# Building the routing tables on GpSimd, reading them in three operations, and splitting the first expert's weights earlier

## The chip, the cores and the metric

The kernel runs on one core of a Trainium2 chip. A core has a matrix engine (TensorE, PE in the profile), a vector engine (VectorE, DVE), a scalar engine (ScalarE, ACT), a general engine (GpSimd, POOL) and SyncE (SP), which here only issues transfers. The engines run side by side, each through its own list of instructions in order, and wait for one another by semaphores. Data lies in HBM, in the on-chip memory SBUF (128 partitions) and in PSUM, where TensorE writes its results. The metric is the device time of one execution in microseconds; lower is better.

## The reference, cut to what matters

```python
B, H, S, D = 8, 8, 576, 64        # attention, window of 64
scores = 0.125 * q @ k.T          # kept where 0 <= row - column < 64
attn = exp(scores - max) / (sum + 1e-9)
x = (attn @ v) as [4608, 512]     # one row per token
logits = x @ w_gate               # 8 experts
e = argmax(logits); gate = softmax(logits)[e]
out[token] = gate * (relu(x @ w1[e]) @ w2[e])   # w1[e]: 512x1024, w2[e]: 1024x512
```

All of it is float32. Each token goes through the one expert that its logits choose, so the kernel must sort tokens by expert.

## The kernel before, in words

**The attention loop.** 4,608 rows are 36 tiles of 128. The main loop runs 43 steps; step i works on several tiles at once, as a pipeline written out by hand: TensorE makes the scores of tile i; VectorE folds them into one window and finds the maximum (`folded`, `largest`); ScalarE takes the exponentials of tile i-1 (`exps`), TensorE transposes them (`transp`), ScalarE copies them out of PSUM (`evac`, tile `tsb`) and GpSimd splits them by two masks (`apart`: two operations `pm` of 128x512, for tile i-2); TensorE multiplies by v (`values`, tile i-3), VectorE divides (`shares`, tile `xrow`, sent to HBM as `xs`), TensorE transposes the rows (`rows_t`, tile i-4), ScalarE copies them (`xT`), and TensorE computes logits. There is one PSUM buffer for most of these, so each engine's list, which is in the order of the code, sets what waits for what. SyncE loads the 72 chunks of q, k and v four steps ahead of their use.

**The routing.** It runs in three rounds, over 14, 12 and 10 tiles. A round (`route`) is a chain of small operations s1 to s8, at most three in a step. s8 ends with each token's place in its expert's list, split into a block number `mid` and a row in the block `lo`, and with the gate `g` split into three bfloat16 parts in `val`. Then `put` makes one-hot rows: `hot_row[:, t]` is 128x128, with a one where the column number equals `lo`. `parts` multiplies, for each wanted block, a mask `here` with five numbers of each token (its partition, its tile, three parts of the gate), giving `said`; TensorE multiplies `said` by `hot_row` (`gathered`, L608), which gives for each place in a block the token and its gate; `read` turns that into an index and a gate. With the index GpSimd gathers rows of `xs` (`fetch`, L172). After round 1 two blocks each of experts 0 and 1 are gathered ahead, after round 2 those of experts 2 and 3; after round 3 a plan is made for all other blocks, with one big table of 32 columns, and passes over them follow until the end.

For round 1, s1 to s3 stand at the end of step 18, s5 to s7 in step 20, s8 and the first two `put`s in step 21, two more `put`s in step 22, `parts` in steps 23 and 24, the table and `read` at the beginning of step 25, the gathers in steps 26 and 27.

**The experts.** From step 29 on TensorE also works on the first expert. Products are made in three passes of single-pass format: a weight tile `raw` is rounded by ScalarE (`whi`, L231) and the remainder taken by VectorE (`wlo`, L228). The first two of these splits for expert 0 are made ahead, each in four pieces of 128x256, one piece in each of steps 20 to 27 (`SPLIT`, `prepare`, `pieces`). Their 8 quarter loads of 256 KB each stand in SyncE's list in steps 18 to 25 (`LOADW`, `quarters`, L850).

## Time and profile before

| what | value |
|---|---|
| median of 3 runs (lowest, highest) | 669.79 us (667.69, 670.86) |
| time of the profiled execution | 670.64 us |
| its span, first to last instruction | 668.8 us |
| PE busy | 618.6 us, 93% |
| DVE busy | 414.2 us, 62% |
| ACT busy | 359.8 us, 54% |
| POOL busy | 193.0 us, 29% |
| DMA | 138.14 MB, mean 207 GB/s |

The attention loop fills the first 205 us or so, mixed with expert work from about 130 us on; from 260 us to the end TensorE works through the experts. A line of the timeline gives start, duration, engine, line of the kernel, operation, what it writes and reads, shapes, and in brackets how long the engine sat idle before it and who ended that. Busy shares are means over stages that have different limits, so a stage is read by itself.

### The profile page before, as it was taken

The numbers are of one execution on the slowest core, as the hardware profiler recorded it, in microseconds if no ns is written. First come the engines' busy times: TensorE is split into PE (matmuls) and PEld (weight loads), VectorE is DVE, ScalarE is ACT, GpSimd is POOL, SyncE is SP. The second block draws the span as 40 slices with busy tenths as digits, with TensorE's granted clock in tenths as the row PEclk, the third lists the DMA queues.
The fourth block names the chain that finished last, engine by engine and source line by source line (L and its number), as shares of the span: only waits on it lengthen the run. The fifth ranks groups of instructions, "written<-read, shape, count | busy, mean of one in ns | idle before, by whom it ended". The sixth has DMA issues, their size and how long they took to land.

```text
span 668.8 us, 17048 instructions
## 1 busy us (share of the span) xinstructions
PE 618.6 (93%) x7001; PEld 545.9 (82%) x7001; DVE 414.2 (62%) x762; ACT 359.8 (54%) x758; POOL 193.0 (29%) x168
## 2 busy tenths in 40 slices
PE   5799968898999899899999999999999999999994
PEld 4677757676777688788999999999999999999994
DVE  4777889765775985554444565555556565555651
ACT  4567655644544354453545555655555555555551
POOL 4565655643443015121111121312212121110011
PEclk9999998998999999999999999999999999999998
DMA  9988887854037346664445676566667657555620
GB/s 313 333 286 253 292 272 232 274 188 159 34 129 283 126 175 246 218 223 153 156 170 175 221 233 213 186 232 236 209 216 244 220 183 239 206 201 188 218 95 34
DMA packets 35111, 138.14 MB, mean 207 GB/s; under 512 B 4940, under 2 KB 6092, under 8 KB 25552
## 3 DMA queue, kind: packets, MB, share of 16 engines
q1 hardware_dynamic: 28624, 118.08, 51.6%
q0 software_dynamic: 6400, 18.88, 8.1%
q8 instruction: 57, 0.93, 0.6%
q14 instruction: 30, 0.25, 0.1%
HBM read 119.11 MB, written 19.92 MB: 208 GB/s over the span
## 4 chain that ended last, share of the span: by engine, by line
PE 74%; DVE 11%; issue 6%; ACT 5%; DMA 2%; POOL 1%; POOLq 0%; DVEq 0%; ACTq 0%
PE s_b L257 14%; PE x_b L257 14%; PE m_b L292 10%; PE t_b L292 9%; PE m_b L296 6%; PE x_b L435 4%; PE t_b L296 4%; PE s_b L378 4%; PE s_b L183 2%; DVE wlo L228 2%; ACT pf L405 2%; PE m_b L452 1%; ACT xT L459 1%; DVE s_b L395 1%; DVE s_b L389 1%
## 5 line engine op out<-in xcount | busy, mean ns | idle before, releaser
L228 DVE TENSOR_TENSOR wlo<-raw,whi 128x1024 fp32r<-128x1024 f32 (+1 forms) x158 | 188.5, 1194 | 164.2 <-ACT whi L231 157.7
L231 ACT CAST whi<-raw 128x1024 fp32r<-128x1024 f32 (+1 forms) x147 | 149.0, 1014 | 99.6 <-PE s_b L257 50.6
L421 POOL TENSOR_TENSOR pm<-tsb,cs 128x512 f32<-128x512 f32 x72 | 91.7, 1296 | 83.0 <-ACT tsb L414 83.0
L265 POOL DMA_INDIRECT out<-ys,idx_sb x32 | 40.7, 1272 | 181.6 <-ACT ys L264 176.7
L172 POOL DMA_INDIRECT xg<-xs,idx_sb x32 | 33.2, 1036 | 156.1 <-PE s_b L183 139.4
L257 PE MATMUL s_b<-whi,hh 128*128 128x512 f32 x176 | 70.1, 398 | 1.7 <-ACT hh L302 1.7
L257 PE MATMUL s_b<-whi,hl 128*128 128x512 f32 x176 | 69.3, 394 | 0.7 <-DVE hl L303 0.6
L257 PE MATMUL s_b<-wlo,hh 128*128 128x512 f32 x176 | 69.0, 392 | 0.0
L405 ACT ACTIVATE pf<-s_b,mxs 128x64 f32<-128x64 f32 x288 | 63.2, 337 | 10.7 <-DVE mxs L397 7.5
L292 PE MATMUL m_b<-xh,whi 128*128 128x256 f32 (+1 forms) x240 | 63.7, 294 | 0.0
L292 PE MATMUL t_b<-xh,whi 128*128 128x256 f32 (+1 forms) x240 | 63.7, 294 | 0.0
L292 PE MATMUL m_b<-xl,whi 128*128 128x256 f32 (+1 forms) x240 | 62.7, 290 | 0.2 <-DVE xl L186 0.2
L292 PE MATMUL t_b<-xl,whi 128*128 128x256 f32 (+1 forms) x240 | 62.5, 289 | 0.0
L302 ACT ACTIVATE hh<-m_b 128x256 fp32r<-128x256 f32 (+1 forms) x82 | 32.6, 398 | 53.8 <-PE m_b L296 53.0
L257 PE MATMUL x_b<-whi,hl 128*128 128x512 f32 x144 | 56.6, 393 | 0.3 <-DVE hl L303 0.3
L257 PE MATMUL x_b<-wlo,hh 128*128 128x512 f32 x144 | 56.5, 392 | 0.0
L257 PE MATMUL x_b<-whi,hh 128*128 128x512 f32 x144 | 56.3, 391 | 0.0
L435 PE MATMUL x_b<-ring,pm 64*64 64x65 f32 x2176 | 46.3, 225 | 8.5 <-issue 4.1
L435 PEld LDWEIGHTS x_b<-ring,pm 64*64 64x64 f32 x2176 | 41.7, 137 | 14.1 <-issue 9.2
L302 ACT ACTIVATE hh<-t_b 128x256 fp32r<-128x256 f32 (+1 forms) x70 | 27.9, 399 | 39.2 <-PE t_b L296 33.4
L303 DVE SCALAR_TENSOR_TENSOR hl<-m_b,hh 128x256 fp32r<-128x256 f32 (+1 forms) x82 | 35.4, 432 | 21.8 <-ACT hh L302 21.0
L378 PE MATMUL s_b<-ring 64*64 64x128 f32 x1024 | 44.3, 292 | 5.0 <-ACT pf L405 2.5
(181 smaller groups left out, 1233.2 us busy)
## 6 DMA issues: line engine op xcount, KB each, us to landing
raw<-wall SPq DMA_DIRECT2D x74, 1024.0 KB, 5.2
ring<-qkv SPq DMA_DIRECT2D x66, 386.0 KB, 4.8
xs<-xrow SPq DMA_DIRECT2D x36, 256.0 KB, 3.4
raw<-wall SPq DMA_DIRECT2D x8, 256.0 KB
ring<-qkv SPq DMA_DIRECT2D x4, 256.0 KB, 4.8
ring<-qkv SPq DMA_DIRECT2D x4, 130.0 KB
ring<-qkv SPq DMA_DIRECT2D x1, 512.0 KB
xg<-xs,idx_sb POOLq DMA_INDIRECT x32
```

Of the source, the lines that this page charges most:

```text
L228: nc.vector.tensor_tensor(out=lo[:, s], in0=raw[:, s], in1=hi[:, s], op=ALU.subtract)
L231: nc.scalar.copy(out=hi[:, s], in_=raw[:, s])
L257: nc.tensor.matmul(y, lhsT=x[:, us], rhs=w[:, C:], start=(j == 0 and m == 0), stop=(j == NJ - 1 and m == 2))
L265: ins = nc.gpsimd.indirect_dma_start(out=out, out_offset=bass.IndirectOffsetOnAxis(ap=ix, axis=0), in_=ys, in_offset=None, bounds_check=N ...
L292: nc.tensor.matmul(hp[:, 0:w], lhsT=hi[:, ks], rhs=x[:, kk, 0:w], start=(kk == 0 and x is xh), stop=False)
L296: nc.tensor.matmul(hp[:, 0:w], lhsT=lo[:, kk * P:(kk + 1) * P], rhs=xh[:, kk, 0:w], start=False, stop=(kk == 3))
L302: nc.scalar.activation(out=hh[:, 0:w], in_=hp[:, 0:w], func=AF.Relu)
L303: nc.vector.scalar_tensor_tensor(out=hl[:, 0:w], in0=hp[:, 0:w], scalar=0.0, in1=hh[:, 0:w], op0=ALU.max, op1=ALU.subtract)
L378: nc.tensor.matmul(sp[cols, a, g], lhsT=q_r[rows, r, g], rhs=k_r[rows, r - 1:r + 1, g], start=True, stop=True)
L405: nc.scalar.activation(out=pf[:, g, a], in_=sp[:, a, g, 0], func=AF.Exp, bias=mx[:, h:h + 1], scale=SCALE)
L421: nc.gpsimd.tensor_tensor(out=pm[i], in0=t.rearrange("p (g q) -> p g q", g=NG), op=ALU.mult, in1=cc("mask")[:, i * P:(i + 1) * P].unsqueez ...
L435: nc.tensor.matmul(x_b[cols, a, g * V1:(g + 1) * V1], lhsT=pm[i][rows, g, cols], rhs=v_r[rows, c % RING - i, g], start=(i == 0), stop=(i = ...
```

## The change

The five parts, in words. (1) The one-hot rows are made by GpSimd, one operation of 128x128 for each tile, instead of by VectorE, four tiles in one operation of 128x512. (2) The four small operations that split the gates move from VectorE to GpSimd. (3) `parts` makes all five products for a small table in one operation (`here` and one product: two operations instead of six); for the large tables it makes five products, the first of which (partition number) was a product with a column before. (4) `read` takes three operations, straight from PSUM, instead of seven; an empty place is now marked by an offset of 256 tiles in `tcol`. (5) Expert 0's first split is prepared from step 12 on (pieces in steps 12 to 19), and its eight quarter loads stand in steps 9, 11, 13, 15 and 20, 22, 24, 26.

```diff
-BIG = float(1 << 20)
+EMPTY = 256
-LOADW = 18
+LOADW = 9
+QUARTERS = ((9, 2), (20, 2))
-SPLIT = 20
+SPLIT = 12
...
-    put("tcol", 1 + np.arange(NT)[None])
+    put("tcol", np.arange(NT)[None] - EMPTY)
...
-                quarters.extend((raw[:, r, a:a + C], src[:, r, a:a + C]) for r in range(2) for a in (0, C))
+                at, gap = QUARTERS[jj]
+                quarters.extend((at + gap * k, raw[:, k // 2, k % 2 * C:(k % 2 + 1) * C],
+                                 src[:, k // 2, k % 2 * C:(k % 2 + 1) * C]) for k in range(4))
...
-            nc.vector.tensor_copy(out=val[:, ts_, 1], in_=v["g"])
-            nc.vector.tensor_tensor(out=new("g1"), in0=v["g"], in1=val[:, ts_, 1], op=ALU.subtract)
-            nc.vector.tensor_copy(out=val[:, ts_, 2], in_=v["g1"])
-            nc.vector.tensor_tensor(out=val[:, ts_, 3], in0=v["g1"], in1=val[:, ts_, 2], op=ALU.subtract)
+            nc.gpsimd.tensor_copy(out=val[:, ts_, 2], in_=v["g"])
+            nc.gpsimd.tensor_tensor(out=new("g1"), in0=v["g"], in1=val[:, ts_, 2], op=ALU.subtract)
+            nc.gpsimd.tensor_copy(out=val[:, ts_, 3], in_=v["g1"])
+            nc.gpsimd.tensor_tensor(out=val[:, ts_, 4], in0=v["g1"], in1=val[:, ts_, 3], op=ALU.subtract)
...
         def put(a, b):
-            nc.vector.tensor_tensor(out=hot_row[:, t0 + a:t0 + b], in0=rowb.unsqueeze(1).to_broadcast([P, b - a, P]),
-                                    in1=v["lo"][:, a:b].unsqueeze(2).to_broadcast([P, b - a, P]), op=ALU.is_equal)
+            for t in range(a, b):
+                nc.gpsimd.tensor_scalar(out=hot_row[:, t0 + t], in0=cc("row"), scalar1=v["lo"][:, t:t + 1], scalar2=None,
+                                        op0=ALU.is_equal)
...
-        for k in (4, 3, 1, 2):
-            nc.vector.tensor_tensor(out=b[:, :, k], in0=here, op=ALU.mult,
-                                    in1=val[:, 0:nt, k - 1].unsqueeze(2).to_broadcast([P, nt, nm]))
+        n = NV if nm < 8 else 1
+        for k in range(0, NV, n):
+            nc.vector.tensor_tensor(out=b[:, :, k:k + n], in0=here.unsqueeze(2).to_broadcast([P, nt, n, nm]), op=ALU.mult,
+                                    in1=val[:, 0:nt, k:k + n].unsqueeze(3).to_broadcast([P, nt, n, nm]))
             yield b
-        nc.vector.tensor_scalar(out=b[:, :, 0], in0=here, scalar1=cc("pcol"), scalar2=None, op0=ALU.mult)
-        yield b
...
-        tt = rt.tile([P, NV, nm], F32, name=f"tt{nm}", bufs=1)
-        nc.vector.tensor_copy(out=tt, in_=tb)
-        nc.vector.tensor_scalar(out=ix, in0=tt[:, 1], scalar1=0.0, scalar2=BIG, op0=ALU.is_equal, op1=ALU.mult)
...
-        nc.vector.tensor_tensor(out=gate, in0=gate, in1=tt[:, 2], op=ALU.add)
+        nc.vector.tensor_scalar(out=ix, in0=tb[:, 1], scalar1=float(P), scalar2=float(P * EMPTY), op0=ALU.mult, op1=ALU.add)
+        nc.vector.tensor_tensor(out=idx, in0=tb[:, 0], in1=ix, op=ALU.add)
+        nc.vector.tensor_reduce(out=gate, in_=tb[:, 2:NV].rearrange("p k m -> p m k"), op=ALU.add, axis=AX.X)
```

What this moves on the engines is shown at three places. GpSimd's list in steps 21 to 23 of the loop, before (`mid` is the end of s7, each pair of `pm` is the mask split of one step):

```order
L562 TENSOR_SCALAR mid<-fl 128x14
L421 TENSOR_TENSOR pm_1926<-tsb,cs_81 128x512
L421 TENSOR_TENSOR pm_1927<-tsb,cs_81 128x512
L421 TENSOR_TENSOR pm_2024<-tsb,cs_81 128x512
L421 TENSOR_TENSOR pm_2025<-tsb,cs_81 128x512
L421 TENSOR_TENSOR pm_2120<-tsb,cs_81 128x512
L421 TENSOR_TENSOR pm_2121<-tsb,cs_81 128x512
```

and now:

```order
L564 TENSOR_SCALAR mid<-fl 128x14
L423 TENSOR_TENSOR pm_1941<-tsb,cs_81 128x512
L423 TENSOR_TENSOR pm_1942<-tsb,cs_81 128x512
L571 CAST val<-g 128x14
L572 TENSOR_TENSOR g_2018<-g,val 128x14
L573 CAST val<-g_2018 128x14
L574 TENSOR_TENSOR val<-g_2018,val 128x14
L586 TENSOR_SCALAR hot_row<-cs_82,lo 128x128 x8
L423 TENSOR_TENSOR pm_2042<-tsb,cs_81 128x512
L423 TENSOR_TENSOR pm_2043<-tsb,cs_81 128x512
L586 TENSOR_SCALAR hot_row<-cs_82,lo 128x128 x6
L423 TENSOR_TENSOR pm_2140<-tsb,cs_81 128x512
```

Twelve operations now stand ahead of the second pair, six more ahead of the third. VectorE's list from s8 at the end of step 21 to the copy of the logits that opens step 22 (`lgT`), before:

```order
L566 SCALAR_TENSOR_TENSOR lo<-mid,pf_1905 128x14
L569 CAST val<-g 128x14
L570 TENSOR_TENSOR g_2004<-g,val 128x14
L571 CAST val<-g_2004 128x14
L572 TENSOR_TENSOR val<-g_2004,val 128x14
L583 TENSOR_TENSOR hot_row<-rowb,lo 128x512 x2
L228 TENSOR_TENSOR wlo<-raw,whi 128x256
L501 COPY lgT<-m_b 128x256
```

and now, with the row ahead and two behind:

```order
L447 TENSOR_TENSOR xrow<-x_b,rs 128x512
L568 SCALAR_TENSOR_TENSOR lo<-mid,pf_1922 128x14
L503 COPY lgT<-m_b 128x256
L390 MEMSET s_b_75 64x8x64
L391 COPY_PREDICATED s_b_75<-fold,s_b_75 128x8x64
```

Between `lo` and `lgT` nothing is left. VectorE's list over the first steps that now make a piece of the split (steps 12 and 13; `lgs` reads the logits, `xrow` is the division):

```order
L487 TENSOR_REDUCE lgs<-x_b 128x16
L230 TENSOR_TENSOR wlo<-raw,whi 128x256
L390 MEMSET s_b_76 64x8x64
L391 COPY_PREDICATED s_b_76<-fold,s_b_76 128x8x64
L397 TENSOR_REDUCE s_b_76<-s_b_76 128x8
L399 TENSOR_SCALAR mxs<-s_b_76 128x8
L443 TENSOR_SCALAR den<-x_b 128x8
L445 RECIPROCAL rs<-den 128x8
L447 TENSOR_TENSOR xrow<-x_b,rs 128x512
L230 TENSOR_TENSOR wlo<-raw,whi 128x256
L503 COPY lgT<-m_b 128x256
```

Before, the same rows stand there without the two `wlo`. On ScalarE a `whi` of 128x256 stands likewise behind each `xT` of steps 12 to 19 and no longer behind those of steps 20 to 27.

## Rows read from the trace of the kernel before

**Rows 1.** Busy time of each engine in stretches of the span: start:end, its length, then us busy (and instructions) of PE, PE's weight loads, DVE, ACT, POOL, then the granted clock of TensorE as a share of full speed, DMA share and GB/s.

```profile
60.00:80.00 20.00, 18.87 (x588) 16.45 (x577) 15.22 (x39) 14.24 (x54) 12.64 (x11) 1.00 0.87 279
...
92.00:104.00 12.00, 7.71 (x170) 6.56 (x172) 11.41 (x26) 5.89 (x22) 5.88 (x5) 0.72 0.63 219
104.00:121.00 17.00, 14.18 (x442) 12.42 (x436) 15.98 (x44) 10.17 (x37) 11.46 (x10) 1.00 0.89 277
...
215.00:236.00 21.00, 17.35 (x103) 14.21 (x104) 19.38 (x69) 6.93 (x12) 0.76 (x3) 1.00 0.38 136
```

**Rows 2.** Waits of TensorE over the whole profile: who waited for whom, us in total, times, longest.

```profile
PE x_b L482 <- DVE lgT L501: 3.7, 1, 3.7
PE x_b L435 <- POOL pm L421: 3.5, 3, 2.2
...
PE x_b L608 <- DVE said L601: 1.4, 1, 1.4
```

**Rows 3.** Timeline of all engines over two undisturbed steps of the loop (steps 16 and 17).

```profile
70.24 0.59 ACT L459 COPY xT<-m_b 128x512 f32<-128x512 f32 x1 [1.52 <-PE m_b L452]
70.73 1.76 ACT L405 ACTIVATE pf<-s_b,mxs 128x64 f32<-128x64 f32 x8
...
72.03 0.70 DVE L389 COPY_PREDICATED s_b<-fold,s_b 128x512 f32<-128x512 int32 x1 [0.84 <-PE s_b L378]
72.31 0.65 ACT L414 COPY tsb<-t_b 128x512 f32<-128x512 f32 x1
...
73.04 2.50 POOL L421 TENSOR_TENSOR pm<-tsb,cs 128x512 f32<-128x512 f32 x2 [1.74 <-ACT tsb L414]
...
77.63 0.59 ACT L459 COPY xT<-m_b 128x512 f32<-128x512 f32 x1 [1.44 <-PE m_b L452]
```

**Rows 4.** Timeline of VectorE from s8 of round 1 (end of step 21) through step 22.

```profile
94.37 0.45 DVE L566 SCALAR_TENSOR_TENSOR lo<-mid,pf 128x14 f32<-128x14 f32 x1
94.74 0.17 DVE L569 CAST val<-g 128x14 bf16<-128x14 f32 x1
...
95.38 0.19 DVE L572 TENSOR_TENSOR val<-g,val 128x14 bf16<-128x14 f32 x1
95.47 2.35 DVE L583 TENSOR_TENSOR hot_row<-rowb,lo 128x512 bf16<-128x512 bf16 x2
97.74 1.48 DVE L228 TENSOR_TENSOR wlo<-raw,whi 128x256 fp32r<-128x256 f32 x1
99.14 0.41 DVE L501 COPY lgT<-m_b 128x256 f32<-128x256 f32 x1
...
102.96 1.02 DVE L583 TENSOR_TENSOR hot_row<-rowb,lo 128x512 bf16<-128x512 bf16 x2
```

**Rows 5.** Timeline of GpSimd: the start, the end of s7 and the mask pairs of steps 21, 22 and 26, the gathers of step 26, and one small operation of round 2.

```profile
0.73 4.01 POOL L355 MEMSET xg<- 128x1536 f32 x3 [0.29 <-POOLq L959]
...
91.54 0.41 POOL L560 TENSOR_SCALAR fl<-pf 128x14 f32<-128x14 f32 x1 [0.21 <-DVE pf L558]
92.04 0.30 POOL L562 TENSOR_SCALAR mid<-fl 128x14 f32<-128x14 f32 x1
92.30 2.49 POOL L421 TENSOR_TENSOR pm<-tsb,cs 128x512 f32<-128x512 f32 x2
95.81 3.13 POOL L421 TENSOR_TENSOR pm<-tsb,cs 128x512 f32<-128x512 f32 x2 [1.02 <-ACT tsb L414]
...
115.48 1.23 POOL L172 DMA_INDIRECT xg<-xs,eidx  x1 [0.18 <-DVE egate L621]
117.02 1.01 POOL L172 DMA_INDIRECT xg<-xs,eidx  x1 [0.31 <-issue]
119.27 2.51 POOL L421 TENSOR_TENSOR pm<-tsb,cs 128x512 f32<-128x512 f32 x2 [1.25 <-ACT tsb L414]
...
173.47 1.19 POOL L560 TENSOR_SCALAR fl<-pf 128x12 f32<-128x12 f32 x1 [0.20 <-DVE pf L558]
```

**Rows 6.** Groups of instructions by line and shape over the whole profile: count, then us busy in all, mean ns of one, and idle time before them.

```profile
L598 DVE TENSOR_TENSOR said<-here,val 128x1152 bf16<-128x1152 bf16 x4 | 5.4, 1350 | 0.0
L228 DVE TENSOR_TENSOR wlo<-raw,whi 128x256 fp32r<-128x256 f32 x8 | 4.7, 592 | 0.4 <-ACT whi L231 0.4
...
L231 ACT CAST whi<-raw 128x256 fp32r<-128x256 f32 x8 | 3.3, 408 | 0.0
...
L601 DVE TENSOR_SCALAR said<-here,cs 128x1152 bf16<-128x1152 bf16 x1 | 0.5, 511 | 0.0
```

**Rows 7.** Timeline of VectorE while the first table is read (step 25; the four rows left out are of 0.15 to 0.17 us each).

```profile
112.03 0.18 DVE L613 COPY tt<-x_b 128x20 f32<-128x20 f32 x1 [0.26 <-PE x_b L608]
...
112.85 1.26 DVE L619 TENSOR_SCALAR eidx<-ix 128x4 int32<-128x4 f32 x1
...
114.21 1.12 DVE L621 TENSOR_TENSOR egate<-egate,tt 128x4 f32<-128x4 f32 x1
```

**Rows 8.** Timeline after round 3: the one-hot rows on VectorE, and TensorE's waits that follow.

```profile
217.80 1.62 DVE L583 TENSOR_TENSOR hot_row<-rowb,lo 128x512 bf16<-128x512 bf16 x3
...
220.61 0.74 PE L296 MATMUL t_b<-xeh,wlo 128*128 128x256 f32 x4 [0.69 <-DVE wlo L228]
...
228.87 0.74 PE L296 MATMUL t_b<-xeh,wlo 128*128 128x256 f32 x4 [1.10 <-DVE wlo L228]
...
232.93 0.42 PE L736 MATMUL s_b<-diag,ones_f 56*128 56x56 f32 x2 [1.09 <-DVE diag L647]
```

More of the change, by code (lines that the diff above doesn't have):

```diff
@@ L164, in window_attention_then_top1_moe @@
     xg = [const.tile([P, WIDE, C], F32, name=f"xg{i}") for i in range(3)]
-    rowb = const.tile([P, P], BF16, name="rowb")
     outs = []
@@ L317, in window_attention_then_top1_moe @@
     hot_row = const.tile([P, NT, P], BF16, name="hot_row")
-    val = const.tile([P, NT, NV - 1], BF16, name="val")
+    val = const.tile([P, NT, NV], BF16, name="val")
     xe = [tuple(const.tile([P, 4, 2 * P], F32R, name=f"{n}{i}") for n in ("xeh", "xel")) for i in range(2)]
@@ L359, in begin_routing @@
         nc.vector.tensor_copy(out=base, in_=cc("ebase"))
-        nc.vector.tensor_copy(out=val[:, :, 0], in_=cc("tcol"))
-        nc.vector.tensor_copy(out=rowb, in_=cc("row"))
+        nc.vector.tensor_copy(out=val[:, :, 0], in_=cc("pcol").to_broadcast([P, NT]))
+        nc.vector.tensor_copy(out=val[:, :, 1], in_=cc("tcol"))
     mxs, pfs, tss, pms, xrs, xps = {}, {}, {}, {}, {}, {}
@@ L611, in read @@
     def read(tb, nm, idx, gate):
-        tt = rt.tile([P, NV, nm], F32, name=f"tt{nm}", bufs=1)
-        nc.vector.tensor_copy(out=tt, in_=tb)
         ix = rt.tile([P, nm], F32, name=f"ix{nm}", bufs=1)
-        nc.vector.tensor_scalar(out=ix, in0=tt[:, 1], scalar1=0.0, scalar2=BIG, op0=ALU.is_equal, op1=ALU.mult)
-        nc.vector.tensor_tensor(out=ix, in0=ix, in1=tt[:, 0], op=ALU.add)
-        nc.vector.scalar_tensor_tensor(out=ix, in0=tt[:, 1], scalar=float(P), in1=ix, op0=ALU.mult, op1=ALU.add)
-        nc.vector.tensor_scalar(out=idx, in0=ix, scalar1=float(-P), scalar2=None, op0=ALU.add)
-        nc.vector.tensor_tensor(out=gate, in0=tt[:, 3], in1=tt[:, 4], op=ALU.add)
-        nc.vector.tensor_tensor(out=gate, in0=gate, in1=tt[:, 2], op=ALU.add)
+        nc.vector.tensor_scalar(out=ix, in0=tb[:, 1], scalar1=float(P), scalar2=float(P * EMPTY), op0=ALU.mult, op1=ALU.add)
+        nc.vector.tensor_tensor(out=idx, in0=tb[:, 0], in1=ix, op=ALU.add)
+        nc.vector.tensor_reduce(out=gate, in_=tb[:, 2:NV].rearrange("p k m -> p m k"), op=ALU.add, axis=AX.X)
     def early_parts(e, nt):
@@ L630, in some @@
                 keep["early"] = next(made[0])
-        return [lambda k=k: some(k) for k in (2, 2, 2)]
+        return [lambda: some(1)] * 2
     def early_table(e, nt):
@@ L813, in window_attention_then_top1_moe @@
             if i == LOADW:
-                ew[0] = Weights(0, 2)
+                ew[0] = Weights(0, len(QUARTERS))
             if i == SPLIT:
@@ L847, in window_attention_then_top1_moe @@
                     load(c)
-            if quarters:
-                o, w = quarters.popleft()
+            if quarters and quarters[0][0] <= i:
+                _, o, w = quarters.popleft()
                 nc.sync.dma_start(out=o, in_=w)
```

## The prediction, before the changed kernel was run

> **What bounds the kernel now.** First I read busy time by stretches, to find where TensorE does not run [rows 1]. From 60 to 80 us, ordinary steps of the loop, TensorE works 18.87 of 20 us; from 92 to 104 us only 7.71 of 12, while VectorE works 11.41; from 104 to 121 us VectorE still has 15.98 of 17; and from 215 to 236 us it has 19.38 of 21 against TensorE's 17.35. These stretches are the tails of routing rounds 1 and 3. Then the waits of TensorE [rows 2]: the longest single one inside the loop, 3.7 us, is for `lgT`, which VectorE copies only after the one-hot rows; another 1.4 us is for `said`. The timelines say why.
>
> Undisturbed steps [rows 3]: from one `xT` to the second after it is 77.63 - 70.24 = 7.4 us, so 3.7 us a step. The cycle that sets this goes through ScalarE's list (`xT` 0.59, exponentials 1.76, `tsb` 0.65), GpSimd (`pm` 2.50), then the products with v, the transposes and the next `xT` on TensorE. VectorE is beside it: it idles 0.84 us before folding. GpSimd idles 1.74 us before the pair shown, but its 2.5 us lie in the cycle.
>
> The end of step 21 [rows 4]: `lo` starts at 94.37, four splits of the gate follow (0.17 to 0.19 us each), two one-hot operations 2.35, one `wlo` 1.48, and only at 99.14 `lgT`. TensorE waits meanwhile, and its granted clock over 92 to 104 us is 0.72 of full speed [rows 1], so part of that stretch ran at 1.2 instead of 2.4 GHz.
>
> **The change part by part.** Terms are worked out against the profiled execution, 670.64 us (span 668.8 and 1.84 around it); the median of the runs is 0.85 lower.
>
> *Round 1, VectorE.* Between `lo` and `lgT` go four splits (about 0.7), the rows (2.35) and the `wlo` (1.48). In step 22 go 1.02 of rows [rows 4], and in each of steps 20 to 27 a `wlo` of 0.59 mean [rows 6]. The read goes from 3.2 us (112.03 to the end of `egate` at 115.33) to three operations of the small rows' 0.2, thus 0.6; two of the seven took 1.26 and 1.12 because GpSimd was in a `pm` pair then, and the new three read PSUM, as does `tt` with 0.18 [rows 7]. The 1.4 us wait for `said` [rows 2] goes too: one product of 280 elements, by 1,350 ns for 1,152 [rows 6] about 0.33 us, now stands a step earlier. So VectorE no longer binds steps 21 to 26.
>
> *Round 1, GpSimd: what is late next.* From the pair of step 21 (92.30) to the end of the pair of step 26 (119.27 + 2.51 = 121.78) GpSimd has six pairs, 15.0 us, and two gathers, 115.48 to 118.03, 2.55 us [rows 5]: 17.55 busy in 29.48. The change queues four small operations and 14 one-hot rows before the pairs of steps 22 and 23, and TensorE's products with v wait behind those pairs. A small one costs 0.3, like `mid` with 0.30 and `fl` with 0.41 [rows 5]: 1.2 in all. An operation of 128x128 with one input and a column of scalars is not in the trace. From below it costs no less than `mid` of 128x14, 0.30. From above, half a `pm` pair is 1.25 us for 512 elements of two inputs, 2.44 ns each, so 114 elements more than `mid` make it 0.30 + 0.28 = 0.58. A wait behind a VectorE operation could make it 1.19, as `fl` took in round 2. The filling of `xg`, 1,336 ns for 1,536 elements [rows 5], is 0.87 ns each and would give 0.40. I take 0.42, by the filling, since it too has fewer than two inputs: 14 x 0.42 = 5.9. GpSimd's sum is then 17.55 + 1.2 + 5.9 = 24.65 us; from 92.30 that ends at 116.95, and with 1.0 us for waits on `tsb` that remain (1.74 before an ordinary pair, rows 3) at 117.95 instead of 121.78: a gain of 3.8. With 0.30 for a row the gain is 5.5, with 0.58 it is 1.6, with 1.19 it is a loss of 6.9. It can't exceed five steps from pair to pair at 3.7: 119.27 - 92.30 - 18.5 = 8.5. TensorE still waits some 3 us in step 23, for `pm` in place of `lgT`, and I keep the half-speed stretch.
>
> *Steps 12 to 19.* Each gets a `whi` (0.41, rows 6) on ScalarE between `xT` and the exponentials, which is inside the two-step cycle: 8 x 0.41 / 2 = 1.6 us. The `wlo` on VectorE (mean 0.59, at most 1.48; rows 4 and 6) has 0.84 us of idle time as cover [rows 3]; where it meets a `pm` pair it overruns, for which I add 0.4: a loss of 2.0. Bounds: 0, if all hides, and 8 x (0.41 + 0.59) = 8.0, if nothing does. What leaves ScalarE in steps 20 to 27 returns nothing, as GpSimd or VectorE binds there.
>
> The Trainium skill's page "SBUF — State Buffer", section "SBUF: two separate sides", has GpSimd and a VectorE operation with two SBUF inputs share one pair of ports by an exclusive lock, held for the whole instruction. The trace agrees: 1.48 us for the `wlo` under a pair [rows 4] against a mean of 0.59 [rows 6]. By it each moved `wlo` would meet a pair with chance 2.5/3.7 and wait half of an operation, 0.6, as an estimate 0.4 us each; were all of that to show, the loss in steps 12 to 19 would be 3.2 us more.
>
> *The eight quarter loads.* Four of 256 KB come to steps 9 to 15, where the transfers take 0.87 of the time [rows 1]. q, k and v are loaded four steps ahead, which hides them; uncovered, each would cost 0.26 MB at 279 GB/s, 0.9 us, or 3.8 for the four. On SyncE each stands behind the two ring loads of its step and ahead of the `xs` write. I take 0.
>
> *Round 2.* The same leaves VectorE (rows and splits about 2.7, the read about 2.6), but TensorE mixes attention and expert work there and GpSimd's pairs lie further apart; I take 0, between a gain of 2 and a loss of 1.
>
> *Round 3.* VectorE is saturated [rows 1] and TensorE waits for it 0.69, 1.10 and 1.09 us after the rows [rows 8]. Rows (1.62) and splits (0.7 as in rows 4) are 2.3 us ahead of all of these. They cover the first two waits and part of the third: a gain of 2.2, at most 2.3; nobody waits for GpSimd's ten rows there, since the big table comes 30 us later. Then the fifth product of the big table becomes 1.35 instead of 0.51 us [rows 6], 0.84 more; VectorE is by then ahead of TensorE, so I take 0 of it, at worst 0.84.
>
> *Sum.* -3.8 + 2.0 + 0 + 0 - 2.2 = -4.0. From 670.64 this is 666.6; measured as a median, 669.79 - 4.0 = 665.8 us.
>
> **The rivals.**
>
> *A. As above, 665.8*, with 663 to 668 as its own range.
>
> *B. A row on GpSimd costs the two-input price, 0.58.* For it: every large GpSimd operation in the trace has two inputs, and comparing may not be the cheap kind. Against it: the filling. The term of round 1 falls to 1.6, the sum to -1.8: 668.0.
>
> *C. GpSimd becomes the bound of steps 21 to 26, slower.* One mechanism: each row waits for VectorE at the shared memory, as `fl` did with 1.19 us [rows 5]. Round 1 loses 6.9, the sum is +6.7: 676.5. It decides from 0.42 + 4.0/14 = 0.71 us a row. Against it: in steps 21 to 23 most of VectorE's work reads PSUM, and the 1.19 stood against one long `wlo` of 128x1024, which round 1 does not have.
>
> *D. The early split costs its full 8.0 us in steps 12 to 19.* The sum is +2.0: 671.8; halfway, at 5.0, 668.8. For it: ScalarE's `whi` is in the cycle. Against it: ScalarE's idle 1.44 and VectorE's 0.84 us a step [rows 3].
>
> *E. More than forecast.* A row costs 0.30 (gain 5.5), half of the `whi` hide (loss 1.0), and the wait for `pm` is short enough for the clock to stay up. In 92 to 104 us the clock's 0.72 means 12 x 0.28 x 2 = 6.7 us at half speed, 3.4 us of TensorE's time; a part of it, 1.5, is taken here, as round 1 can't give more than 8.5. The sum is -5.5 + 1.0 - 1.5 - 2.2 = -8.2: 661.6.
>
> **How the numbers follow.** Chances: A 0.49, B 0.14, C 0.09, D 0.08, E 0.20. The time is A's, 665.8. About 0.5% (3.3 us, so below 666.4 or above 673.1) is what a measurement of this kernel tells from no change. A lies close to that bound, so 0.33 of its 0.49 counts as faster; with E and 0.02 of B that is 0.55. C and 0.03 of D are slower: 0.12. The rest, 0.33, is no change. The range reaches from somewhat below E's time, 660.5, to 670.5, which takes in A, B and half of D; C, the worst of D and the tail of E are left out, together under 0.2.
>
> **What would show each step.** `lgT` behind `lo` with nothing between, and TensorE's 3.7 us wait for it gone; in its place a wait of the products with v for `pm` in step 23, with eight `hot_row` of 0.4 us ahead of the pair on GpSimd. The distance from the pair of step 21 to the end of that of step 26 at about 25.6 instead of 29.48 us. The read at 0.6 us, no wait for `said`. Two steps at 7.4 us in 60 to 80 us becoming about 7.9. In round 3 the waits of 0.69 and 1.10 gone. The prediction is wrong if a row on GpSimd takes over 0.7 us, if steps 12 to 19 grow by over 0.5 us each, or if a half-speed stretch of TensorE appears or goes that has no wait of these parts before it.

## The result: 0.84% slower

| what | before | after |
|---|---|---|
| median of 5 runs each (lowest, highest) | 668.24 us (667.69, 670.86) | 673.63 us (670.34, 675.81) |
| ratio after / before, with its 95% interval | | 1.0084 (1.0057 to 1.0111) |
| span of the profiled execution | 668.8 us | 668.6 us |

Predicted were a gain and 665.8 us, in a range of 660.5 to 670.5. The profile after is of the quickest of the five executions, so it understates the loss; where something went is read by stages. A stage is measured here by the division `xrow`, which VectorE does once a step (the k-th one belongs to step k+2): the length of steps 23 and 24 is the time from the `xrow` of step 22 to that of step 24.

GpSimd's timeline in the profile after, from the mask pair of step 21 to the gathers, answers to [rows 5]:

```profile
95.52 2.50 POOL L423 TENSOR_TENSOR pm<-tsb,cs 128x512 f32<-128x512 f32 x2
97.97 0.22 POOL L571 CAST val<-g 128x14 bf16<-128x14 f32 x1
...
99.05 4.67 POOL L586 TENSOR_SCALAR hot_row<-cs,lo 128x128 bf16<-128x128 f32 x8
103.69 2.48 POOL L423 TENSOR_TENSOR pm<-tsb,cs 128x512 f32<-128x512 f32 x2
106.15 3.49 POOL L586 TENSOR_SCALAR hot_row<-cs,lo 128x128 bf16<-128x128 f32 x6
109.60 4.96 POOL L423 TENSOR_TENSOR pm<-tsb,cs 128x512 f32<-128x512 f32 x4
119.12 2.49 POOL L423 TENSOR_TENSOR pm<-tsb,cs 128x512 f32<-128x512 f32 x2 [4.57 <-ACT tsb L416]
...
124.37 2.50 POOL L423 TENSOR_TENSOR pm<-tsb,cs 128x512 f32<-128x512 f32 x2
```

Fourteen rows take 8.2 us. The pairs of steps 23 and 24 then run back to back (`x4`), and before the pair of step 25 GpSimd idles 4.57 us. From the pair of step 21 to the end of that of step 26 it is 124.37 + 2.50 - 95.52 = 31.35 us, against 29.48 before. What held the `tsb` of step 25 stands in VectorE's timeline of the same steps, which answers to [rows 4] and, in its last three rows, to [rows 7]:

```profile
97.51 0.54 DVE L568 SCALAR_TENSOR_TENSOR lo<-mid,pf 128x14 f32<-128x14 f32 x1
97.97 0.41 DVE L503 COPY lgT<-m_b 128x256 f32<-128x256 f32 x1
...
108.52 0.69 DVE L447 TENSOR_TENSOR xrow<-x_b,rs 128x512 f32<-128x512 f32 x1
109.13 0.34 DVE L597 TENSOR_TENSOR here<-mid,cs 128x56 bf16<-128x56 f32 x1
109.58 5.28 DVE L602 TENSOR_TENSOR said<-here,val 128x280 bf16<-128x280 bf16 x1
114.79 0.41 DVE L503 COPY lgT<-m_b 128x256 f32<-128x256 f32 x1
...
118.49 0.17 DVE L616 TENSOR_SCALAR ix<-x_b 128x4 f32<-128x4 f32 x1 [0.59 <-PE x_b L610]
118.69 0.16 DVE L617 TENSOR_TENSOR eidx<-x_b,ix 128x4 int32<-128x4 f32 x1
118.77 0.16 DVE L618 TENSOR_REDUCE egate<-x_b 128x4 f32<-128x12 f32 x1
```

At the end of step 21 `lgT` stands right behind `lo`, and the three operations of the read take 0.16 to 0.17 us each, 0.5 in all. But the product `said` of step 23 takes 5.28 us: it begins as GpSimd begins its four mask operations (109.60) and ends 0.3 us after they end (114.56). This is called the shut-out below. All of VectorE's list stands behind it, the next `lgT` first. TensorE's waits in the profile after, answering to [rows 2] (total, times, longest in us; those for `pm` in the first 110 us):

```profile
PE x_b L437 <- POOL pm L423: 4.5, 3, 3.6
...
PE x_b L484 <- DVE lgT L503: 1.9, 1, 1.9
```

The same waits on TensorE's timeline:

```profile
105.00 0.49 PE L437 MATMUL x_b<-ring,pm 64*64 64x65 f32 x8 [3.61 <-POOL pm L423]
106.22 1.79 PE L437 MATMUL x_b<-ring,pm 64*64 64x65 f32 x56 [0.73 <-POOL pm L423]
...
115.25 0.44 PE L484 MATMUL x_b<-cs,lgT 128*128 128x128 f32 x2 [1.92 <-DVE lgT L503]
...
117.95 0.50 PE L610 MATMUL x_b<-said,hot_row 128*128 128x20 bf16 x14 [1.39 <-DVE lgs L487]
```

The 3.7 us wait for `lgT` in step 22 has become 3.61 + 0.73 for `pm` in step 23, and a wait of 1.92 for `lgT` has been added a step later. The stretches of [rows 1], in the profile after:

```profile
60.00:80.00 20.00, 18.50 (x554) 15.65 (x547) 16.57 (x40) 14.32 (x54) 13.32 (x12) 1.00 0.89 299
92.00:104.00 12.00, 9.16 (x251) 7.76 (x249) 10.32 (x30) 8.32 (x30) 10.26 (x20) 1.00 0.86 278
104.00:121.00 17.00, 11.96 (x294) 10.49 (x295) 11.25 (x18) 5.51 (x20) 12.43 (x14) 0.80 0.52 163
215.00:236.00 21.00, 18.92 (x115) 15.72 (x115) 18.44 (x62) 8.13 (x15) 9.24 (x17) 0.92 0.46 171
```

The idle stretch of TensorE has moved, and with it the lower clock: 0.72 in 92 to 104 us before, 0.80 in 104 to 121 us now.

### The profile page after: what moved, and what is told of

It is laid out like the page before. It is cut to its first block, busy times and chain, and to the rows that moved or that the text cites. A ratio compares the mean times of both kernels' runs of the same rounds, so it can differ in the third digit from the quotient of the medians.

```text
span 668.6 us, 17054 instructions
## 1 busy us (share of the span) xinstructions
PE 621.9 (93%) x7001; PEld 548.9 (82%) x7001; DVE 405.0 (61%) x720; ACT 359.3 (54%) x758; POOL 219.3 (33%) x216
## 4 chain that ended last, share of the span: by engine, by line
PE 71%; DVE 10%; issue 8%; POOL 6%; ACT 3%; DMA 1%; POOLq 0%; DVEq 0%; ACTq 0%
PE s_b L259 14%; PE x_b L259 14%; PE m_b L294 11%; PE t_b L294 9%; PE m_b L298 5%; POOL pm L423 5%; PE t_b L298 5%; PE s_b L380 3%; PE x_b L437 3%; PE s_b L183 2%; DVE wlo L230 1%; ACT pf L407 1%; DVE said L602 1%; DMA ring<-qkv 1%; DVE xrow L447 1%
## 5 line engine op out<-in xcount | busy, mean ns | idle before, releaser
L233 ACT CAST whi<-raw 128x1024 fp32r<-128x1024 f32 (+1 forms) x147 | 149.3, 1016 | 103.2 <-PE s_b L259 51.2
L380 PE MATMUL s_b<-ring 64*64 64x128 f32 x1024 | 46.8, 304 | 4.3 <-ACT pf L407 2.5
L294 PEld LDWEIGHTS m_b<-xl,whi 128*128 128x128 f32 x240 | 45.2, 188 | 2.3 <-DVE xl L186 0.6
```

The lines of the kernel that those rows point to most:

```text
L233: nc.scalar.copy(out=hi[:, s], in_=raw[:, s])
L294: nc.tensor.matmul(hp[:, 0:w], lhsT=hi[:, ks], rhs=x[:, kk, 0:w], start=(kk == 0 and x is xh), stop=False)
L380: nc.tensor.matmul(sp[cols, a, g], lhsT=q_r[rows, r, g], rhs=k_r[rows, r - 1:r + 1, g], start=True, stop=True)
```

## The experiments

Five sets, each on one chip (the second and the fourth on the same one) with the kernel before run in between; every time of a changed kernel is a median of 12 runs, and the kernel before has its median, over 23 or 35 runs, in the same set. Stage lengths come from the one profile of each kernel in each set. Single executions of one and the same kernel lie up to 10 us apart, so only the ratios, with their intervals, decide on times.

**First set: parts taken away from the change** (kernel before 670.09 us). First the kernel after again, unchanged.

> The changed kernel, unchanged, once more. Both theories: a median near 673.6 us and runs spread over some 5 us. The rows theory (the loss is made in steps 21 to 24 by the one-hot rows on GpSimd: 0.60 us each ahead of the mask pairs, and the product of 280 elements shut out behind pairs that then follow each other without a gap) expects the product at over 3 us again and a wait of the products with v for pm of 3 to 4 us. The split theory (the loss is made in steps 12 to 19) expects these steps at 2.5 to 3.5 us longer than before in every profile, and whatever happens later to vary.

Then the rows and splits back on VectorE, in all rounds:

```diff
-            nc.gpsimd.tensor_copy(out=val[:, ts_, 2], in_=v["g"])
+            nc.vector.tensor_copy(out=val[:, ts_, 2], in_=v["g"])
...
-            for t in range(a, b):
-                nc.gpsimd.tensor_scalar(out=hot_row[:, t0 + t], in0=cc("row"), scalar1=v["lo"][:, t:t + 1], scalar2=None,
-                                        op0=ALU.is_equal)
+            nc.vector.tensor_tensor(out=hot_row[:, t0 + a:t0 + b], in0=rowb.unsqueeze(1).to_broadcast([P, b - a, P]),
+                                    in1=v["lo"][:, a:b].unsqueeze(2).to_broadcast([P, b - a, P]), op=ALU.is_equal)
```

> The changed kernel with the one-hot rows and the four small splits back on VectorE (parts 1 and 2 undone). Rows theory: the wait for pm in step 22 and the long product go, and with the shorter read left the time is 666 to 668 us, not slower than before. Split theory: the loss of steps 12 to 19 stays, 670 to 673 us.

The early split undone, and both of these undone, which leaves the products and the read:

```diff
-LOADW = 9
-QUARTERS = ((9, 2), (20, 2))
+LOADW = 18
+QUARTERS = ((18, 1), (22, 1))
-SPLIT = 12
+SPLIT = 20
```

> The changed kernel with the split and its loads back in steps 20 to 27 and 18 to 25 (part 5 undone). Rows theory: steps 12 to 19 return to before, 2 to 3 us better, the rest stays or gets worse since the wlo pieces join the locked-out steps: 670 to 673 us. Split theory: 666 to 668 us.

> The kernel before with the two operations of parts and the three of read alone (parts 3 and 4). Both theories: faster than before by the 3 us that the read loses in step 25, some of which returns as a wait for pm: 664.5 to 667 us. If it is not faster than before, the read was not on the path that sets the end.

Measured: after again 671.36 us, 1.003 (0.9999 to 1.0061); rows back 670.67, 0.9999 (0.9969 to 1.003); split late 670.99, 1.0018 (0.9995 to 1.0041); products and read alone 670.50, 1.0018 (0.9994 to 1.0042). None of them is told from the kernel before, so the times of this set do not decide between the two theories; what the read alone was to bring did not come, and the 673.6 us that both theories expected of the kernel after did not return. The shut-out did: in the profile of the kernel after, `said` took 5.29 us. The stages are clearer and stand in the table behind the fourth set.

**Second set: parts put alone into the kernel before** (666.35 us): part 5, parts 1 and 2, and the kernel before itself, for a second profile; and a candidate, the kernel after with the split late and with the rows and splits of round 1 on VectorE.

> The kernel before with part 5 alone (pieces of the first split in steps 12 to 19, quarter loads in steps 9 to 15 and 20 to 26). Theory 1, the early split is paid in its own steps: steps 12 to 19 take 35.5 to 38.5 us, as in the three kernels with part 5 so far, instead of 33.0; steps 20 to 26 get at most 2 us shorter, since VectorE loses a wlo of 0.6 in each; the time is 0 to 3 us above the kernel before. Theory 2, the spread of single executions made that difference: steps 12 to 19 stay within 0.7 us of 33.0, and the gain of steps 20 to 26 shows as a time 1 to 3 us lower.

> The kernel before with parts 1 and 2 alone (one-hot rows and splits of the gates on GpSimd; products and read as before). Theory 1: a row takes 0.60 us, fourteen of them 8.2, so GpSimd sets steps 21 to 24; steps 20 to 26 take 38 to 40 us against 36.6, and one of the small products of VectorE is shut out by the mask operations for over 1.5 us; the time is 1 to 4 us above the kernel before. Theory 2, rows on GpSimd are harmless and the slow step is the one with the product over all five parts: no product over 0.8 us, steps 20 to 26 take 34 to 36.6 us, and the time is 1 to 3 us lower.

> The kernel before, unchanged, for a second profile of it. Theory 1, stage lengths belong to the kernel: steps 3 to 11, 12 to 19 and 20 to 26 take 31.6, 33.0 and 36.6 us again within 0.7 us each, the wait of 3.7 us for lgT is there, and the clock falls in step 22. Theory 2, they belong to the execution: one of the three stages moves by over 1.5 us and half-speed stretches lie elsewhere.

> The kernel after with part 5 undone and with rows and splits on VectorE in round 1, on GpSimd only in rounds 2 and 3. Theory 1, round 1 on GpSimd and the early split are what the change loses: steps 12 to 19 take 33 us, steps 20 to 26 35 to 36.5, the rest as in the kernel after; the time is 1 to 3 us below the kernel before. Rival: the read of 0.5 us is given back in the gathers' steps and rows on GpSimd gain nothing in rounds 2 and 3 either: within 1 us of the kernel before.

Measured: the split early alone 665.66, 0.9978 (0.9956 to 0.9999); rows and splits on GpSimd alone 670.41, 1.0055 (1.0033 to 1.0077); before again 666.23, 0.9995 (0.9973 to 1.0016), with steps 4 to 11, 12 to 19 and 20 to 26 at 30.0, 33.0 and 36.3 us: in the first profile the two stages that the change touches had 33.0 and 36.6, and what came earlier moved by 1.6. The stages of other kernels vary more: three profiles of the early split alone, over the sets, have 35.1, 32.2 and 36.3 us in steps 12 to 19. The candidate 666.43, 0.9999 (0.9977 to 1.0021), no gain. With parts 1 and 2 alone, GpSimd's timeline shows the pairs of steps 23 to 25:

```profile
107.73 5.10 POOL L419 TENSOR_TENSOR pm<-tsb,cs 128x512 f32<-128x512 f32 x4
117.51 2.49 POOL L419 TENSOR_TENSOR pm<-tsb,cs 128x512 f32<-128x512 f32 x2 [4.68 <-ACT tsb L412]
```

and VectorE's timeline beside it:

```profile
107.72 3.96 DVE L597 TENSOR_TENSOR said<-here,val 128x56 bf16<-128x56 bf16 x3
111.61 1.50 DVE L227 TENSOR_TENSOR wlo<-raw,whi 128x256 fp32r<-128x256 f32 x1
113.04 0.41 DVE L499 COPY lgT<-m_b 128x256 f32<-128x256 f32 x1
```

The old, separate products are shut out too (3.96 us for three, which take 0.2 each where GpSimd is idle), and a `wlo` with them (1.50 us). The form of the product is not what shuts it out. Steps 20 to 26 take 40.3 us: theory 1 of this kernel held, in the stages and in the time.

**Third set: is the shut-out product the cause?** (667.92 us.) In the kernel after, `here` and `said` of round 1 are moved from step 23 to the end of step 24, with the table still at the start of step 25:

```diff
-                puts.extend(early_parts(e0, rows))
-                puts.append(lambda: begin.extend(
+                here, said = early_parts(e0, rows)
+                table = lambda: begin.extend(
...
+                puts.extend([lambda: None, lambda: None, here, lambda: (said(), table())] if rnd == 0 else [here, said, table])
```

> The kernel after with one thing moved: in round 1 the mask and the product for the small table stand at the end of step 24 instead of step 23, so that no VectorE operation with two operands in SBUF stands among the four mask operations that GpSimd runs in a row; the table keeps its place at the start of step 25. Theory 1, the shut-out product is what makes GpSimd's rows lose: the product takes 0.45 us, the wait of 1.9 us for lgT goes, steps 23 and 24 take 12.5 to 14 us together instead of 16.1, and the time is 2 to 4 us below the kernel after run beside it. Rival, GpSimd's 8.2 us of rows and the wait for pm in step 23 set these steps: steps 23 and 24 stay at 15.5 us or more, and the time is within 1 us of the kernel after.

> The kernel after, unchanged, beside the others on the same chip. Both theories: 0.2 to 0.9% above the kernel before; steps 12 to 19 take 35 to 38.5 us and steps 20 to 26 38.5 to 40, with a product of over 4 us in step 23.

Measured: product late 670.83, 1.0035 (1.0006 to 1.0064); after 672.11, 1.0082 (1.0047 to 1.0117). With the product late, VectorE's timeline shows

```profile
106.77 0.42 DVE L503 COPY lgT<-m_b 128x256 f32<-128x256 f32 x1 [1.84 <-PE m_b L502]
...
111.04 0.45 DVE L603 TENSOR_TENSOR said<-here,val 128x280 bf16<-128x280 bf16 x1
```

and steps 23 and 24 take 13.2 us together against 16.0 in the first profile of the kernel after. So the 5.28 us and the wait for `lgT` are gone, as theory 1 says; the gain of 2 to 4 us over the kernel after that it expected did not come. But the profile of the kernel after in this set shows that the shut-out comes and goes, first in VectorE's timeline:

```profile
107.35 0.69 DVE L447 TENSOR_TENSOR xrow<-x_b,rs 128x512 f32<-128x512 f32 x1
107.96 0.20 DVE L597 TENSOR_TENSOR here<-mid,cs 128x56 bf16<-128x56 f32 x1
108.27 0.47 DVE L602 TENSOR_TENSOR said<-here,val 128x280 bf16<-128x280 bf16 x1
```

and then in GpSimd's, the pairs of steps 23 and 24:

```profile
109.18 4.96 POOL L423 TENSOR_TENSOR pm<-tsb,cs 128x512 f32<-128x512 f32 x4
```

Here the product began 0.9 us ahead of the four mask operations and took 0.47; steps 23 and 24 took 13.2 us. The expectation of a product over 4 us fell. The two kernels differ by 1.3 us in their medians, and their intervals overlap. The shut-out adds 2.8 us to steps 23 and 24; that it costs the whole execution as much is not shown: over steps 20 to 26 the profile with it is 1.5 us longer (38.6 against 37.2), over steps 20 to 28 it is 1.1 us shorter (49.3 against 50.4), as the other has a stretch of 3.4 us at half speed in step 27. How often it happens is not known; of the six profiles with round 1's rows on GpSimd and the product in step 23, five show it, with 2.84 to 5.29 us. Without it the rows still cost something: steps 20 to 26 take 37.2 us in both profiles, as against 32.5 to 35.0 with the same early split and rows on VectorE.

Two candidates ran in the same set: part 5 with the rows of rounds 2 and 3 on GpSimd, and that with the new products and read.

> The kernel before with part 5 and with rows and splits on GpSimd in rounds 2 and 3 alone (products and read as before, round 1 on VectorE). Theory 1, the parts' effects add: part 5 gave -0.2%, rows in the later rounds give up to -2 us by the waits after round 3, so 2 to 4 us below the kernel before. Rival, rows in the later rounds are hidden: as part 5 alone, 0.5 to 1.5 us below.

> As the kernel with part 5 and late rows, with the new products and the new read too (the kernel after with only round 1's rows and splits back on VectorE). Theory 1, the faster read of round 1 is given back by the gathers, which GpSimd starts only after its mask pair: within 1 us of the kernel with part 5 and late rows, with step 25 some 2 us shorter and steps 26 to 28 some 2 us longer. Rival, the read is worth its 2.6 us once VectorE no longer makes the pieces there: 2 to 3 us below it.

Measured: 670.40, 1.0025 (0.9999 to 1.0052), and 671.48, 1.0032 (1.0001 to 1.0063). Neither gains; that they add up was wrong. The second of them is the kernel after with nothing but round 1's rows and splits put back on VectorE: 1.0032 against 1.0082 on the same chip, but with intervals that overlap, and the kernel with the product late, 1.0035, is no slower than it.

**Fourth set: the four pieces one at a time on one chip** (666.98 us). The rows and splits of round 1 alone on GpSimd, those of rounds 2 and 3 alone, and part 5 and the read again. The edit, here for round 1:

```diff
+            eng = nc.vector if rnd else nc.gpsimd
-            nc.vector.tensor_copy(out=val[:, ts_, 1], in_=v["g"])
+            eng.tensor_copy(out=val[:, ts_, 1], in_=v["g"])
...
+            if rnd:
...
+                return
+            for t in range(a, b):
+                nc.gpsimd.tensor_scalar(out=hot_row[:, t0 + t], in0=cc("row"), scalar1=v["lo"][:, t:t + 1], scalar2=None,
+                                        op0=ALU.is_equal)
```

> The kernel before with rows and splits of round 1 alone on GpSimd. Theory 1, round 1 pays: eight rows ahead of the mask pair of step 22 and six ahead of that of step 23 put a wait of about 3.5 us for pm in place of the wait for lgT, and steps 20 to 26 take 38.5 to 40.5 us against 36.5; the time is 2 to 4 us above the kernel before. Rival, the later rounds pay: within 1 us of it.

> The kernel before with rows and splits of rounds 2 and 3 alone on GpSimd. Theory 1: rounds 2 and 3 have slack on GpSimd, so nothing is lost, and at most 2.2 us are gained by VectorE's shorter work after round 3: 2 us below the kernel before to 0.5 above. Rival, the later rounds pay (small operations of GpSimd and VectorE in each other's way): 1.5 to 3 us above it.

> The early split alone, again, beside the other parts on one chip. Theory 1: steps 12 to 19 take 35 to 36 us against 33, steps 20 to 26 34 to 35 against 36.5, and the time is 2 us below the kernel before to 0.5 above. Rival, it pays in full: 1 to 3 us above.

> The products and the read alone, again, beside the other parts on one chip. Theory 1, the gathers of step 26 stand behind GpSimd's mask pair of step 25 with the old read as with the new, so step 25 gets 2.5 us shorter and steps 26 to 28 as much longer: within 1.5 us of the kernel before. Rival, the read is worth its time: 2 to 3 us below it.

Measured: round 1 alone 670.65, 1.0039 (1.0017 to 1.0061); later rounds alone 666.39, 0.9982 (0.9958 to 1.0005); early split 665.24, 0.9969 (0.9946 to 0.9992); products and read 665.21, 0.9976 (0.9953 to 0.9999). Round 1 pays for the rows, the later rounds do not. The expectation of the early split's stages fell: its profile has 32.2 us in steps 12 to 19, not 35 to 36. The stages by where round 1's rows are made and when the split is made (means in us over the profiles of all sets, in brackets their number; left out is the kernel after in the first set, whose profiled execution, 678.75 us, was the longest of its twelve, with 38.4 and 40.0 us in these stages):

| round 1's rows | split | steps 12 to 19 | steps 20 to 26 |
|---|---|---|---|
| VectorE | late | 33.1 (6) | 35.8 (6) |
| VectorE | early | 35.1 (7) | 34.2 (7) |
| GpSimd | late | 33.9 (3) | 39.8 (3) |
| GpSimd | early | 34.7 (3) | 37.7 (3) |

Rows on GpSimd add 4.0 us to steps 20 to 26 with the late split, 3.5 with the early one (the kernel with the product late counts there). The rows of the table mix the old read with the new one, which shortens step 25; among kernels with the same read the rows add 3.6 to 4.0. The early split adds 0.8 to 2.0 in steps 12 to 19, where single profiles of one cell lie up to 5.5 us apart, and takes back 1.6 to 2.1 in steps 20 to 26. Steps 27 to 38 take 81.2 us on average with GpSimd's rows and 81.7 with VectorE's, and 79 to 85 in single profiles: a loss that comes back later is not seen.

The clock could be a rival here, as the kernels with GpSimd's rows spend more of these steps at half speed. Here are steps 20 to 26 of the kernel after (its first profile), of that with the product late, and of that with round 1's rows on VectorE (third set); the third number from the end is the granted clock:

```profile
86.81:125.45 38.64, 29.77 (x781) 26.29 (x780) 27.94 (x64) 19.11 (x71) 27.88 (x36) 0.87 0.64 201
83.00:120.19 37.19, 29.37 (x782) 25.06 (x781) 23.90 (x65) 19.13 (x71) 29.95 (x38) 0.91 0.71 229
86.82:121.49 34.67, 29.15 (x781) 25.58 (x780) 26.87 (x72) 19.18 (x71) 21.13 (x19) 0.90 0.74 240
```

The last two spend nearly the same time at half speed (length x (1 - clock) x 2: 6.7 and 6.9 us), and the rows still cost 2.5 us; in all five profiles with the early split, VectorE's rows and 6.9 to 7.0 us at half speed these steps take 34.3 to 35.0. The first spends 10.0, so a part of its further 1.5 us goes with the clock. With the late split no two profiles can be set side by side in this way: the three with GpSimd's rows have 10.2 to 10.5 us at half speed, the six with VectorE's 3.6 to 7.0. The 5 us between their means are 2.5 us of TensorE's time, so by this estimate up to 2.5 of the 4.0 us may go with the clock; whether the rows cause it is not shown.

**Fifth set: adding or not** (667.67 us), the early split and the combination of all but round 1's rows.

> The early split alone, for the third time. Theory 1, its gain belongs to the kernel: 0.2 to 0.3% below the kernel before on any chip. Rival, it belongs to the chip of the earlier sets: within 0.1% of the kernel before, or above it.

> Early split, late rows, new products and read together (the kernel after with round 1's rows and splits on VectorE), again, beside the early split alone. If the parts add: 0.6 to 0.8% below the kernel before. If they are in each other's way: no better than the early split alone, whichever way that goes.

Measured: 667.99, 1.0002 (0.9982 to 1.0023), and 667.30, 0.9984 (0.9959 to 1.0009). On this chip the split gains nothing. The versions without round 1's rows on GpSimd lie between 0.9969 and 1.0032 over the sets. Four of their intervals leave out 1 by a little (the early split twice and the read once below it, the combination of the third set above it), but none of these came again in another set: 1.0002, 1.0018 and 0.9984 there. All kernels with these rows lie above 1: 1.0084, 1.0030, 1.0082, 1.0018, 1.0055, 1.0035 and 1.0039; in the first set (1.0030 and 1.0018) the interval holds 1. The clearest times are those of the second and fourth sets, on one chip: 1.0055 and 1.0039 with the rows, 0.9969 to 0.9999 without. On the chip of the third set versions without them reach 1.0025 and 1.0032, so there the times alone do not single out the rows.

## Why the prediction was wrong, step by step

**Round 1 on GpSimd, predicted as a gain of 3.8 us, is a loss of 3.5 to 4.0 in steps 20 to 26.** This is the step that failed, in two terms. The row: "I take 0.42, by the filling"; it measured (4.67 + 3.49) / 14 = 0.58 in the profile after, the two-input price of rival B. By the prediction's own sum that would still have been a gain, 1.6. The larger fault is in the other term, "with 1.0 us for waits on `tsb` that remain". GpSimd does not work off a sum here: it is one link of a ring, and when it falls behind, the next `tsb` is late too. In place of 1.0 us it idled 4.57 before the pair of step 25, and 2.26 in the profiles without the shut-out. Span from pair 21 to the end of pair 26: 25.6 predicted, 31.35 in the profile after, 29.1 with the product late (117.80 + 2.51 - 91.22), 29.48 before. Of the 5.7 us between 25.6 and 31.35 the rows are 2.3 (8.2 in place of 5.9) and the waits 3.6 (4.57 in place of 1.0). Without the shut-out the span comes out as before, with the rows paid and VectorE's wait saved. One reading of the prediction was off without harm: the six pairs that it puts at 15.0 us took 15.6 before (that of step 22 took 3.13), and 14.9 after. The old read took 3.3 us, not 3.2.

Where the idle time is doubled, it follows the shut-out: it is 2.26 and 2.27 us in the two profiles without it, 3.27 in the two in which the products took 2.84 and 2.94, and 4.57 to 4.68 in the three in which they took 3.96 to 5.29. The prediction had seen that contention from one side only: it let a VectorE operation be lengthened by a pair (1.48 us for a `wlo`, rows 4) and let a row wait for VectorE (rival C), but not a VectorE operation wait for a chain of GpSimd's. The Trainium skill's page "SBUF — State Buffer", section "SBUF: two separate sides", says that whoever starts first holds the shared ports for the whole instruction and the other blocks. The trace agrees on the blocking, and goes beyond it: with four mask operations in a row the product waited for all four, 5.28 us, where one of them takes 1.24.

Rival C had the sign and the place right (GpSimd becomes the bound of steps 21 to 26), but not the mechanism: its price of over 0.71 us a row did not come about, and the loss came without it.

**`lgT` right behind `lo`, the wait for `pm` in step 23, the read at 0.5 us without a wait for `said` before it: right**, except that the rows ahead of the pair took 0.58 and that TensorE still waited 1.39 us ahead of the table, now for `lgs`, which stood behind the shut-out product. The half-speed stretch was kept, as predicted: granted clock 0.50 from 97.3 to 104.1 us before, and from 105.0 to 111.8 after. But it is not of one size in a kernel: in the second profile of the kernel before, and in that of the kernel after in the third set, it is half as long (99.8 to 103.2, and 106.4 to 109.8). And the profile after has 3.4 us more of it in step 20 (87.9 to 91.3), which neither profile of the kernel before has; it begins behind a wait of TensorE for `xrow` that took 2.29 us, against 1.15 before.

**Steps 12 to 19, a loss of 2.0: right in size**, 0.8 to 2.0 over the profiles, as far as their spread lets one tell. "What leaves ScalarE in steps 20 to 27 returns nothing" was wrong: 1.6 to 2.1 us come back there. So part 5 is worth little, and its times agree: 0.9978, 0.9969, 1.0002. The eight loads cost 0, as taken: from 20 to 100 us no wait of TensorE is for a load, before or after.

**The read.** It shortens step 25 by 2.7 us, from 7.13 to 4.45, in the kernel with products and read alone; steps 26 to 28 take 18.6 us there against 13.6 before, and in its second profile 15.0 against 13.4. Why nothing is gained stands in GpSimd's timeline of that kernel:

```profile
112.96 2.51 POOL L425 TENSOR_TENSOR pm<-tsb,cs 128x512 f32<-128x512 f32 x2 [1.55 <-ACT tsb L418]
115.63 1.23 POOL L173 DMA_INDIRECT xg<-xs,eidx  x1 [0.16 <-issue]
117.17 1.00 POOL L173 DMA_INDIRECT xg<-xs,eidx  x1 [0.31 <-issue]
118.19 2.52 POOL L425 TENSOR_TENSOR pm<-tsb,cs 128x512 f32<-128x512 f32 x2
```

The gate and the index are ready 2.8 us earlier (112.55 against 115.33), but the gathers begin at 115.63, as before at 115.48, because the pair of step 25 stands ahead of them; and the next pair stands behind them. That steps 26 to 28 lose more than step 25 gains is not explained by this. A part goes with the clock: 0.91 over these steps in the first profile, 1.00 in the second. It is not this kernel's alone: in the eleven profiles with the new read steps 26 to 28 take 17.0 us on average (14.5 to 19.0), in the nine with the old one 13.8 (13.4 to 14.3), while step 25 takes 4.7 against 6.9. The prediction counted the read as a part of VectorE's relief and asked whom it frees, but not what stands ahead of the gathers on GpSimd.

**Round 3, a gain of 2.2: half of it came.** From the matmul of the masks `oh`, which TensorE starts at 212.81 us before, to that of `diag` at 232.93 [rows 8] it is 20.1 us. In the kernel with the later rounds' rows alone TensorE's timeline shows

```profile
213.67 0.20 PE L534 MATMUL x_b<-oh,tri 128*128 128x88 bf16 x1 [0.99 <-DVE oh L529]
...
228.61 0.74 PE L296 MATMUL t_b<-xeh,wlo 128*128 128x256 f32 x4 [1.53 <-DVE wlo L228]
232.66 0.43 PE L742 MATMUL s_b<-diag,ones_f 56*128 56x56 f32 x2 [1.08 <-DVE diag L653]
```

which is 19.0 us, so 1.1 are won (the second profile of the kernel before has 20.1 again). The wait of 0.69 [rows 8] is gone, that of 1.10 has become 1.53, and the one of 1.09 stays at 1.08: VectorE still comes last. Of the 2.3 us of work that leave it, 1.1 remain won by the time it makes `diag` (14.5 us after `lo`, against 15.6 before); beside the ten rows, which run on GpSimd from 219.76 to 226.50, its small operations take up to 0.34 us where they took 0.17. Measured: 0.9982 (0.9958 to 1.0005), in which 1.1 us has room, and no gain too.

**The sum.** Put right by the table it is (34.7 + 37.7) - (33.1 + 35.8) = +3.5 us for round 1 and the split together, 0 for the read and for round 2 (the read's times are 1.0018 and 0.9976), and -1.1 for round 3: +2.4 us, thus 0.4%, at the lower end of what the kernel after shows (0.3, 0.82 and 0.84%). Of the bounds that the prediction named, a loss needed a row of over 0.71 us; the loss came at 0.58, with the wait for the ring.

**Open.** The pieces one at a time on one chip sum to -0.34%, the whole is +0.3 to +0.84%. Round 1's rows alone cost 0.39% of it (0.55% with those of the later rounds). The whole did not run on that chip, so whether the rest is an interaction, the chip, or the clock (below) is not settled.

## What to carry to other kernels

Work moved to an engine that is one link of a ring is paid as it delays that link, not as a share of its idle time: 9 us of small operations on an engine with 12 us idle cost 4. Before moving work that reads SBUF to GpSimd, look at which operations with two SBUF operands VectorE issues while GpSimd will run several in a row (here `said`, 0.45 or 5.28 us), and keep them out of that stretch; what this gains in time was too small to be told here. A read that gets faster gains only from the point at which whatever consumes it is free to start.

## What the runs showed that was not expected

A product of 0.45 us that takes 5.28 when it begins with four queued GpSimd operations, and 0.47 when it begins 0.9 us ahead of them, within the same program. And the part of an execution that TensorE spends at the lower level of its clock, 1.2 in place of 2.4 GHz, which moves from one execution to another of the same kernel. Here are three stretches of two profiled executions of one kernel, the combination of all but round 1's rows, first in the fifth set, span 659.4 us:

```profile
0.00:65.00 65.00, 53.10 (x1490) 44.91 (x1490) 44.72 (x110) 40.37 (x150) 36.66 (x33) 1.00 0.91 314
65.00:130.00 65.00, 53.84 (x1516) 45.20 (x1514) 51.14 (x135) 41.44 (x150) 42.18 (x36) 1.00 0.84 271
130.00:195.00 65.00, 58.53 (x1149) 48.43 (x1148) 40.27 (x94) 32.66 (x94) 35.78 (x39) 0.97 0.38 129
```

The same stretches in the third set, on another chip, span 670.2 us:

```profile
0.00:65.00 65.00, 53.80 (x1402) 45.68 (x1406) 43.67 (x107) 38.37 (x141) 36.21 (x33) 0.97 0.90 303
65.00:130.00 65.00, 53.51 (x1457) 45.25 (x1449) 50.48 (x128) 39.23 (x145) 39.20 (x34) 0.94 0.79 258
130.00:195.00 65.00, 57.89 (x1090) 47.42 (x1087) 38.31 (x92) 33.85 (x104) 32.71 (x37) 0.93 0.41 137
```

The first has 3.9 us at half speed in its first 195, the second 20.8 (65 x (1 - clock) x 2, summed). Which part of that is cause and which follows from waits was not separated; it is why a change of 4 us needs many runs of both kernels on one chip.
